# Second MLP of a fused kernel: ScalarE alone empties the product banks, VectorE makes all the splits, and the output weight's sums come one per block product

## The chip, the cores and the metric

The kernel runs on one core of a Trainium2 chip, as one program. The time is the device time of that program in microseconds (us). Before the change it took 1174.68 us, the median of 3 runs (1170.27 to 1175.73). The profiled execution, from which all rows below come, took 1168.19 us; 1166.4 us of it lie between its first and its last instruction (its span).

## The reference, cut to what matters

The program computes three things in a row: attention with RMS norms over 4 batches of 448 tokens, a first MLP without a nonlinearity, and a second MLP. The change touches the second MLP alone. Its reference, for x of 1792 tokens by 768:

```python
h = x @ w_in                      # 768 x 2048
relu6 = np.clip(h + 3.0, 0.0, 6.0)
g = h * relu6 / 6.0
return (g @ w_out).astype(np.float32)   # 2048 x 768
```

## The kernel before, in words

All matmuls run in a reduced-precision type (float32r), so each float32 operand is split in two: a rounded "high" part, made by a ScalarE copy, and the remainder, made by a subtraction of the copy from the original. A product is then three matmuls: high by high, high by low, low by high.

The second MLP works on two pairs of batches (p = 0, then p = 1). Both of its matrix products use Strassen's scheme with seven block products instead of eight. The items of work stand in one list, in the order of `ORDER`. A block, j = 0 to 7 in each pair, has the seven products P1, P2, P6, P5, P7, P3, P4 of x with w_in (nine matmuls of 448 columns each), with the items O2 and O1 of earlier blocks between them (nine matmuls each into six accumulator banks, the tiles `acc`). When all eight blocks of a pair are done, 40 more such `acc` items follow, the rest of the product with w_out. So each pair has 8 x 7 x 9 matmuls into the banks `sA` and `sB`, and 56 x 9 into `acc`.

`sA` and `sB` are used in turn, and a bank's later products are added to what it holds (P6, P7 and P4 add to P1's bank). TensorE may therefore start a product only after the one before it in the same bank has been read out. Some results are read by a ScalarE copy to a tile `u` in SBUF (P1, P6, P5, L1263), some by a VectorE addition straight out of the bank (P2, P7, P3, L1271), and P4 by the two steps of the nonlinearity (`nonlinear`, L1193 on ScalarE and L1194 on VectorE). `gsplit` (L1201) splits what the nonlinearity gives, and `three` and `fourth` (L1225 to L1237) form Strassen's combinations of it on VectorE.

`halves` (L1016) splits the weights (tiles `wt`, 128x384) and the pieces of x (tiles `xo`, 128x448): ScalarE copies, and the subtraction goes to VectorE and GpSimd in turn by the counter `nsplit`, with some weights on VectorE always. `temp` (L1136) forms the sums of w_in (tiles `sx`), and `combos` (L1102) forms the four sums of a w_out block (tiles `G`), all four in one go, and stores them (`sd`) for the 40 later items. `outer` also empties the `acc` banks at the end of a group, partly by VectorE additions out of PSUM.

`prepare` runs six items ahead of the matmuls. The program text is in this order, but a scheduling pass places the instructions on each engine; after that an engine takes its own strictly in order. The loop over the items is the last one below.

```python
    def halves(t, src, alone=False):
        nc.scalar.activation(t[:, 0, :], src, AF.Copy)
        nsplit[0] += 1
        (nc.vector if nsplit[0] % 2 or alone else nc.gpsimd).tensor_sub(t[:, 1, :], src, t[:, 0, :])
```

Of the kernel before, what the change touches and what calls it, by code (L numbers as in the profile page):

```python
# [13 lines left out]
F32 = mybir.dt.float32  # L14
F32R = mybir.dt.float32r
# [3 lines left out]
AF = mybir.ActivationFunctionType  # L19
# [8 lines left out]
P = 128  # L28
# [9 lines left out]
NH = DM // 2  # L38
# [13 lines left out]
def fused_kernel(ctx: ExitStack, tc: tile.TileContext, nat, qT, kT, vin, gq, gk,  # L52
                 w12, w3t, wo, win, wo2, outT):
    nc = tc.nc
# [52 lines left out]
    now = [0]  # L107
# [813 lines left out]
    NWF, NWT, AHEAD2 = 12, 8, 6  # L921
    PAIRS = ((0, 1), (2, 3))
    d1 = ExitStack()
    mp = d1.enter_context(tc.tile_pool(name="m2", bufs=1, side="left", **RW))
    wf, wr, xo = {}, {}, {}
# [81 lines left out]
    def utile():  # L1007
        return mp.tile([P, S], F32, tag="u", bufs=8, name="u")

    def xtile(z, k):  # L1010
        return xo["pool", z in LEFT].tile([P, 2, S], F32R, tag=f"x{z}{k}", name="xo")

    LEFT = ("11", "21", "T2", "T1", "T3")
    nsplit = [0]

    def halves(t, src, alone=False):  # L1016
        nc.scalar.activation(t[:, 0, :], src, AF.Copy)  # L1017
        nsplit[0] += 1
        (nc.vector if nsplit[0] % 2 or alone else nc.gpsimd).tensor_sub(t[:, 1, :], src, t[:, 0, :])
        return t  # L1020

    def xprep(p):
# [59 lines left out]
            items += dn[-2:]  # L1082
        base += 3 * NJ
    wt, sx, once = {}, {}, set()
    wait, puts = [], []

    def drop2(v):
        if v in once:
            drop(v)
        once.add(v)  # L1090

    def combos(j, v1, v2):
        w1, w2 = wf[v1], wf[v2]
        a11, a21 = w1[:, :NH], w1[:, NH:]
        a12, a22 = w2[:, :NH], w2[:, NH:]
        s, t = [], []
        for n, op in enumerate((ALU.add, ALU.subtract, ALU.subtract, ALU.subtract)):
            if n % 2 == 0:
                t.append(xo["pool", False].tile([P, 2, S], F32, tag="G", bufs=M2 // 2, name="G"))
            s.append(t[-1][:, n % 2, :NH])  # L1100
            x, y = ((a21, a22), (s[0], a11), (a11, a21), (a12, s[min(n, 1)]))[n]
            nc.vector.tensor_tensor(out=s[n], in0=x, in1=y, op=op)  # L1102
        drop2(v1)
        drop2(v2)

        def keep():
            for n in range(2):
                dma(sd[j, n], t[n][:, :, :NH])
            made.add(j)

        puts.append((now[0] + 3, keep))

    def prepare(i):
        kind, p, j, v, h = items[i]
        front[0] = v if kind == "O" else v[1]
        if kind == "O":
            upto(v)
            c = slice(NH, 2 * NH) if h in "634" else slice(0, NH)
            wt[i] = halves(mp.tile([P, 2, NH], F32R, tag="wt", bufs=NWT, name="wt"), wf[v][:, c], h not in "12")
            if h in "534":  # L1120
                drop(v)
            elif h in "12" and p == 0:
                drop2(v)
                if h == "1":
                    upto(v + 1)
                    wait.append((now[0], partial(combos, j, v, v + 1)))
            elif h in "12":
                drop(v)
            return
        upto(v[1])  # L1130
        a11, a12 = wf[v[0]][:, :NH], wf[v[0]][:, NH:]
        a21, a22 = wf[v[1]][:, :NH], wf[v[1]][:, NH:]

        def temp(z, x, y, op):
            sx[z] = mp.tile([P, NH], F32, tag="sx", bufs=3, name="sx")
            nc.vector.tensor_tensor(out=sx[z], in0=x, in1=y, op=op)  # L1136
            return sx[z]

        if kind == "P6":
            temp("S1", a21, a22, ALU.add)  # L1140
            temp("S2", sx["S1"], a11, ALU.subtract)
        src = dict(P1=a11, P2=a12, P4=a22).get(kind)
        if src is None:
            if kind == "P7":
                src = temp("S3", a11, a21, ALU.subtract)
            elif kind == "P3":
                src = temp("S4", a12, sx["S2"], ALU.subtract)
            else:
                src = sx["S2" if kind == "P6" else "S1"]
        t = mp.tile([P, 2, NH], F32R, tag="wt", bufs=NWT, name="wt")  # L1150
        wt[i] = halves(t, src)
        if h:
            drop(v[0])
            drop(v[1])
# [33 lines left out]
    xo["pool", False] = rp  # L1188
    rp.tile([P, 2, S], F32, tag="G", bufs=M2 // 2, name="G")

    def nonlinear(src, out):
        u = utile()
        nc.scalar.activation(u, src, AF.Relu, bias=half, scale=1.0 / 6.0)  # L1193
        return nc.vector.scalar_tensor_tensor(out=u if out is None else out, in0=u, scalar=1.0, in1=src,  # L1194
                                              op0=ALU.min, op1=ALU.mult), u

    g, done = {}, []
# [3 lines left out]
        done[:] = [nc.scalar.activation(t[:, 0, :], src, AF.Copy), nc.vector.tensor_sub(t[:, 1, :], src, t[:, 0, :])]  # L1201
        g[p, b, q] = t

    def finish(p, j, z, src):

        b, q = (z % 10 - 1), 2 * j + z // 10 - 1
        if b == 0:
            _, u = nonlinear(src, None)
            gsplit(p, 0, q, u)
            X[z] = u  # L1210
            if z == 21:
                wait.append((now[0] + 2, partial(fourth, j)))
        elif z == 22:
            X["b"] = rp.tile([P, 2, S], F32, tag="G", bufs=M2 // 2, name="G")
            nonlinear(src, X["b"][:, 1])
        else:
            _, X[z] = nonlinear(src, None)
            wait.append((now[0] + 2, partial(three, j)))

    X = {}  # L1220
# [20 lines left out]
    swap = [(sA, sB)]  # L1241
    snap = {}
# [12 lines left out]
    def strassen(i):  # L1255
        kind, p, j, _, _ = items[i]
        a, c = swap[0]
        own = c if kind in ("P2", "P5", "P3") else a
        snap["mm"] = product(kind, i, own, kind in ("P1", "P2", "P5"))
        r = own[:, :S]  # L1260
        if kind in ("P1", "P6", "P5"):
            snap[kind] = utile()
            nc.scalar.activation(snap[kind], r, AF.Copy)  # L1263
            return
        if kind == "P4":
            finish(p, j, 21, r)
            swap[0] = (c, a)
            return
        s, z = {"P2": ("P1", 11), "P7": ("P5", 22), "P3": ("P6", 12)}[kind]
        s = snap.pop(s)  # L1270
        nc.vector.tensor_add(s, r, s)  # L1271
        finish(p, j, z, s)

    acc = {}

# [23 lines left out]
    def outer(i):  # L1299
        _, p, j, _, h = items[i]  # L1300
        if not acc:
            for n in range(KD):
                acc[n] = bank(TAGS[1 + n // 2], "acc")
        low = 3 * (h in "253")
        w = wt.pop(i)
        x = g.pop((p, 0, 2 * j + int(h) - 1) if h in "12" else (p, h, j))
        first, end = j == 0 and h in "1253", j == NJ - 1
        for n in range(3):
            ps, ns = acc[low + n][:, :S], slice(n * P, n * P + P)
            with tc.issue_after(snap["mm"].ins) if i >= turn[p] - 2 else ExitStack():  # L1310
                for a, (y, z) in enumerate(((0, 0), (0, 1), (1, 0))):
                    nc.tensor.matmul(ps, w[:, y, ns], x[:, z, :], start=first and a == 0, stop=end and a == 2,  # L1312
                                     skip_group_check=h in "674")
        if not end:
            return
        b1, b2 = PAIRS[p]

        def put(n, b, t):
            dma(outT[n * P : n * P + P, b * S : b * S + S], t)

        for n in range(3):
            ps = acc[low + n][:, :S]
            if h == "1":
                snap["c", n] = utile()
                nc.scalar.activation(snap["c", n], ps, AF.Copy)
            elif h == "2":
                t = snap["c", n]
                nc.vector.tensor_add(t, ps, t)
                put(n, b1, t)
            elif h == "6":  # L1330
                snap["o", n] = xtile("22", n).bitcast(F32)
                nc.scalar.activation(snap["o", n][:, 1], ps, AF.Copy)
            elif h == "5":
                t = snap["o", n]
                nc.scalar.activation(t[:, 0], ps, AF.Copy)
                nc.vector.tensor_add(t[:, 1], ps, t[:, 1])
            elif h == "4":
                t = utile()
                if n % 2:
                    nc.vector.tensor_copy(t, ps)  # L1340
                else:
                    nc.scalar.activation(t, ps, AF.Copy)
                put(n + 3, b1, t)
            else:
                t = utile()
                nc.vector.tensor_add(t, ps, snap["o", n][:, int(h == "3")])
                put(n + 3 * (h == "7"), b2, t)

    prep_to(AHEAD2)
    xg = xrest(0)  # L1350
    for i, it in enumerate(items):
# [5 lines left out]
        kind, p = it[:2]  # L1357
# [19 lines left out]
        (outer if kind == "O" else strassen)(i)  # L1377
        while puts and puts[0][0] <= i:
            puts.pop(0)[1]()
        while wait and wait[0][0] <= i:  # L1380
            with tc.issue_after(done[1].ins):
                wait.pop(0)[1]()
# [47 lines left out]
```

## Time and profile before

| what | value |
|---|---|
| median of 3 runs | 1174.68 us |
| profiled execution, its time | 1168.19 us |
| its span | 1166.4 us |
| TensorE matmul (PE) busy | 1111.8 us, 95% of the span |
| weight loads (PEld) busy | 943.0 us, 81% |
| VectorE (DVE) busy | 930.2 us, 80% |
| ScalarE (ACT) busy | 778.7 us, 67% |
| GpSimd (POOL) busy | 297.9 us, 26% |
| mean granted TensorE clock | 0.997 of full speed |

The second MLP's matmuls begin at 732.15 us and end near the end of the span, so it takes the last 434 us. A matmul's recorded time (367 ns or so) overlaps the next one's; the pace of a dense stream is read from how far apart the weight loads start, or from a long stretch divided by its matmuls. Each row of waits names the engine and line that waited, and after the arrow the engine and line whose end released it, then the total in us, the number of waits and the longest one. In rows of groups, "x16 | 12.1, 754 | 0.0" means 16 instructions, 12.1 us busy together, 754 ns each on average, and the engine's idle time just before them.

### The profile page before, as it was taken

Reading aid. Unit: us, or ns where it says so; the run is one execution under the profiler, and the core shown is the slowest. Engines: PE = TensorE matmul, PEld = TensorE weight load, DVE = VectorE, ACT = ScalarE, POOL = GpSimd, SP = SyncE. Lnnn points to the kernel's source line nnn. Section 1 sums busy time; section 2 is a strip of 40 time slices with the busy share of each in tenths; the row PEclk is TensorE's granted clock in tenths of the full one; section 3 lists DMA queues with packets and bytes.
Section 4 is the critical chain, followed back from the end, with each engine's and each line's share of the span. In section 5 each row is a group of like instructions: output and inputs, shape, how many; then the busy total and the mean of one; then the engine's idle time right before and its main releaser. Section 6 shows DMA issues by size and latency. Waiting matters only on the chain.

```text
span 1166.4 us, 17544 instructions
## 1 busy us (share of the span) xinstructions
PE 1111.8 (95%) x5483; PEld 943.0 (81%) x5483; DVE 930.2 (80%) x1956; ACT 778.7 (67%) x1645; POOL 297.9 (26%) x249
## 2 busy tenths in 40 slices
PE   5899899899999999999999999899999989999998
PEld 2455576788789888788999899889889879999997
DVE  6869888989788898878874436898989997777764
ACT  6988968898678878777764434545556755555663
POOL 1132322645322213222102004423310253222000
PEclk9999999999999999999999999999999999999999
DMA  8989744789999889898689987654459954434961
GB/s 263 341 273 292 255 142 151 239 285 285 331 309 339 280 295 316 271 314 281 232 295 338 398 315 278 233 194 176 153 205 402 355 174 149 150 129 163 349 230 72
DMA packets 109662, 299.05 MB, mean 256 GB/s; under 512 B 13280, under 2 KB 46048, under 8 KB 109568
## 3 DMA queue, kind: packets, MB, share of 16 engines
q1 hardware_dynamic: 109568, 297.93, 74.4%
q8 instruction: 43, 0.70, 0.3%
q14 instruction: 51, 0.42, 0.1%
HBM read 230.61 MB, written 67.27 MB: 255 GB/s over the span
## 4 chain that ended last, share of the span: by engine, by line
PE 46%; DVE 21%; DMA 16%; ACT 11%; issue 5%; POOL 1%; SPq 0%; ACTq 0%; DVEq 0%; POOLq 0%
PE acc L1312 11%; PE sA L1251 5%; PE sB L1251 5%; PE bank L395 5%; PE bank L256 4%; DMA raw<-in_wo_dram 3%; DMA nat<-in_nat_dram 3%; PE bank L400 2%; DVE PP L638 2%; PE bank L657 2%; ACT PP L650 2%; PE bank L91 2%; PE bank L89 2%; PE bank L90 2%; DVE xl L676 2%
## 5 line engine op out<-in xcount | busy, mean ns | idle before, releaser
L1312 PE MATMUL acc<-g,wt 128*128 128x448 f32 x1008 | 217.0, 368 | 2.5 <-DVE g L1201 2.2
L1312 PEld LDWEIGHTS acc<-g,wt 128*128 128x128 f32 x1008 | 189.1, 188 | 21.8 <-DVE g L1201 3.5
L395 PE MATMUL bank<-xhl,ws 128*128 128x448 f32 x768 | 180.9, 367 | 2.4 <-ACT bs L371 1.2
L395 PEld LDWEIGHTS bank<-xhl,ws 128*128 128x128 f32 x768 | 143.6, 188 | 15.8 <-ACT bs L416 1.6
L650 ACT ACTIVATE PP<-PP,mx 112x448 f32<-112x448 f32 x192 | 127.0, 663 | 36.5 <-DVE mx L645 32.9
L638 DVE CUSTOM_DVE_ANT_0 PP<-bank,rb,rq 112x448 f32<-112x448 f32 x192 | 128.6, 674 | 12.9 <-PE bank L632 10.1
L1251 PE MATMUL sA<-xo,wt 128*128 128x448 f32 x504 | 114.2, 371 | 9.0 <-DVE u L1271 7.8
L256 PE MATMUL bank<-woh,w 128*128 128x384 f32 x256 | 98.6, 509 | 15.3 <-DVE woh L155 12.8
L1251 PE MATMUL sB<-xo,wt 128*128 128x448 f32 x504 | 112.6, 367 | 0.0
L1251 PEld LDWEIGHTS sA<-xo,wt 128*128 128x128 f32 x504 | 94.8, 190 | 20.6 <-DVE u L1271 11.1
L1251 PEld LDWEIGHTS sB<-xo,wt 128*128 128x128 f32 x504 | 93.9, 188 | 10.1 <-DVE u L1271 1.6
L657 PEld LDWEIGHTS bank<-ident,PP 112*128 112x128 f32 x672 | 78.2, 141 | 28.7 <-issue 7.5
L676 DVE TENSOR_TENSOR xl<-bank,xh 128x448 fp32r<-128x448 f32 x142 | 86.9, 615 | 16.5 <-ACT xh L666 15.4
L666 ACT ACTIVATE xh<-bank 128x448 fp32r<-128x448 f32 (+1 forms) x156 | 82.4, 536 | 25.9 <-PE bank L657 23.0
L152 DVE SCALAR_TENSOR_TENSOR raw<-raw 128x384 int32<-128x384 int32 (+1 forms) x112 | 69.4, 620 | 37.4 <-ACT raw L150 33.4
L657 PE MATMUL bank<-ident,PP 112*128 112x112 f32 x672 | 94.4, 262 | 3.4 <-DVE xl L676 2.5
L400 PE MATMUL bank<-xhl,ws 128*128 128x448 f32 x384 | 94.7, 366 | 0.0
L149 ACT ACTIVATE raw<-raw 128x384 f32<-128x384 f32 (+1 forms) x112 | 63.6, 568 | 40.7 <-DMA raw<-in_wo_dram 16.2
L1017 ACT ACTIVATE wt<-wf 128x384 fp32r<-128x384 f32 x160 | 79.2, 514 | 15.1 <-PE sB L1251 6.8
L631 PE MATMUL bank<-K,Q 128*112 128x448 f32 x192 | 79.9, 417 | 5.9 <-DVE mx L638 5.9
L256 PEld LDWEIGHTS bank<-woh,w 128*128 128x128 f32 x256 | 48.8, 196 | 43.8 <-DVE woh L155 16.0
L612 POOL TENSOR_TENSOR K<-kr,K 128x448 fp32r<-128x448 f32 x48 | 59.7, 1264 | 77.5 <-ACT K L610 65.1
(146 smaller groups left out, 2275.7 us busy)
## 6 DMA issues: line engine op xcount, KB each, us to landing
ws<-w12d SPq DMA_DIRECT2D x48, 768.0 KB
ws<-wpd SPq DMA_DIRECT2D x32, 768.0 KB
wf<-wfd SPq DMA_DIRECT2D x56, 384.0 KB
raw<-in_wo_dram SPq DMA_DIRECT2D x44, 384.0 KB
td<-G SPq DMA_DIRECT2D x32, 448.0 KB
G<-td SPq DMA_DIRECT2D x32, 448.0 KB
raw<-in_w_dram SPq DMA_DIRECT2D x32, 384.0 KB
w12d<-ws SPq DMA_DIRECT2D x16, 768.0 KB
```

The costliest lines, as they stand in the source:

```text
L256: nc.tensor.matmul(ps[:, :NH], W["w3"][a, c // 4][:, cs], W["woh"][c, n], start=c == 0, stop=c == M1 - 1)
L395: nc.tensor.matmul(ps[:, :S], w[:, 0, ks], x[:, y, :], start=k == 0 and y == 0, stop=False)
L400: nc.tensor.matmul(ps[:, :S], w[:, 1, ks], L["xhl"][i][:, 0, :], start=False, stop=k == KD - 1)
L631: nc.tensor.matmul(ps[:CP, :S], qs, k1[:, j, :], start=True, stop=False)
L638: anchors[8 * i + s].append(nc.vector.tensor_tensor_reduce(out=T["PP", i][:, c, sl], in0=ps[:CP, :S], in1=T["rb", i][:, sl], op0=ALU.mult, ...
L650: anchors[8 * i + s].append(nc.scalar.activation(v, v, AF.Exp, bias=T["m", i][:, 8 + s : 9 + s], accum_out=T["sum", i][:, s : s + 1]))
L657: nc.tensor.transpose(ps[:, c * CP : c * CP + CP], src[:, c, kb * P : kb * P + P], ident[:CP, :CP])
L666: nc.scalar.activation(hi, ps, AF.Copy)
L676: nc.vector.tensor_sub(lo, ps, hi)
L1017: nc.scalar.activation(t[:, 0, :], src, AF.Copy)
L1251: mm = nc.tensor.matmul(ps[:, :S], w[:, a, ks], x[:, c, :], start=first and k == 0 and n == 0, stop=k == KD // 2 - 1 and n == 2, skip_grou ...
L1312: nc.tensor.matmul(ps, w[:, y, ns], x[:, z, :], start=first and a == 0, stop=end and a == 2, skip_group_check=h in "674")
```

## The change

Five edits, all in the second MLP.

1. `halves` has no counter any more: VectorE makes every remainder, and GpSimd has no work in this part.
2. In `strassen` ScalarE copies each of the seven products out of its bank into a `u` tile. The additions of P2, P7 and P3 and both steps of P4's nonlinearity then read SBUF. `nonlinear` is handed the tile for its intermediate instead of taking one.
3. In `outer` each finished `acc` bank is likewise copied by ScalarE, and VectorE's additions read the copy.
4. `combos` is a generator: its four sums are emitted one after each item of the list, not four at once, each placed behind the latest `gsplit`.
5. The two weight tiles that `combos` reads are given back, and its sums stored, as many items later.

```diff
-    def halves(t, src, alone=False):
+    def halves(t, src):
         nc.scalar.activation(t[:, 0, :], src, AF.Copy)
-        nsplit[0] += 1
-        (nc.vector if nsplit[0] % 2 or alone else nc.gpsimd).tensor_sub(t[:, 1, :], src, t[:, 0, :])
+        nc.vector.tensor_sub(t[:, 1, :], src, t[:, 0, :])
...
-            s.append(t[-1][:, n % 2, :NH])
-            x, y = ((a21, a22), (s[0], a11), (a11, a21), (a12, s[min(n, 1)]))[n]
-            nc.vector.tensor_tensor(out=s[n], in0=x, in1=y, op=op)
+            x, y = ((a21, a22), (t[0][:, 0, :NH], a11), (a11, a21), (a12, t[0][:, 1, :NH]))[n]
+            nc.vector.tensor_tensor(out=t[-1][:, n % 2, :NH], in0=x, in1=y, op=op)
+            yield
...
-                    wait.append((now[0], partial(combos, j, v, v + 1)))
+                    sums.append(combos(j, v, v + 1))
...
         r = own[:, :S]
+        c = utile()
+        nc.scalar.activation(c, r, AF.Copy)
         if kind in ("P1", "P6", "P5"):
-            snap[kind] = utile()
-            nc.scalar.activation(snap[kind], r, AF.Copy)
+            snap[kind] = c
             return
         if kind == "P4":
-            finish(p, j, 21, r)
-            swap[0] = (c, a)
+            finish(p, j, 21, c, utile())
+            swap[0] = swap[0][::-1]
             return
...
-        nc.vector.tensor_add(s, r, s)
-        finish(p, j, z, s)
+        nc.vector.tensor_add(s, c, s)
+        finish(p, j, z, s, c)
...
+            t = utile()
+            nc.scalar.activation(t, ps, AF.Copy)
+            if h == "2":
+                nc.vector.tensor_add(t, t, snap["c", n])
+            elif h in "73":
+                nc.vector.tensor_add(t, t, snap["o", n][:, int(h == "3")])
+            put(n + 3 * (h in "74"), b2 if h in "73" else b1, t)
...
+        with tc.issue_after(done[1].ins) if done else ExitStack():
+            while sums and next(sums[0], 0) == 0:
+                sums.pop(0)
```

The scheduling pass gives a new order on each engine. The first place is VectorE in the middle of pair 0, around the four sums of one block of w_out (`G<-wf` and the like) and the two additions of P7 and P3 behind them (`u<-sA,u` and `u<-sB,u` before, `u<-u` now). Before:

```order
L1201 TENSOR_TENSOR g<-u,g 128x448
L1237 TENSOR_TENSOR u<-u,G 128x448
L1102 TENSOR_TENSOR G<-wf 128x384 x2
L1102 TENSOR_TENSOR G<-G,wf 128x384
L1102 TENSOR_TENSOR G<-wf,G 128x384
L1019 TENSOR_TENSOR wt<-sx,wt 128x384
L1136 TENSOR_TENSOR sx<-wf,sx 128x384
L1136 TENSOR_TENSOR sx<-wf 128x384
L1271 TENSOR_TENSOR u<-sA,u 128x448
L1136 TENSOR_TENSOR sx<-sx,wf 128x384
L1271 TENSOR_TENSOR u<-sB,u 128x448
```

and the same place now:

```order
L1197 TENSOR_TENSOR g<-u,g 128x448
L1233 TENSOR_TENSOR u<-u,G 128x448
L1098 TENSOR_TENSOR G<-wf 128x384 x2
L1016 TENSOR_TENSOR wt<-sx,wt 128x384
L1098 TENSOR_TENSOR G<-G,wf 128x384
L1016 TENSOR_TENSOR wt<-sx,wt 128x384
L1133 TENSOR_TENSOR sx<-wf,sx 128x384
L1098 TENSOR_TENSOR G<-wf,G 128x384
L1133 TENSOR_TENSOR sx<-wf 128x384
L1268 TENSOR_TENSOR u<-u 128x448
L1016 TENSOR_TENSOR wt<-sx,wt 128x384
L1133 TENSOR_TENSOR sx<-sx,wf 128x384
```

The four sums are loosened by weight splits, of which there are more; the addition of P7 still stands behind all four, but it no longer reads a bank.

The second place is ScalarE where the second MLP begins: the first block's copies out of `sA` and `sB`, and the six copies of pieces of x that are split late (`xo<-wr`). Before:

```order
L1263 ACTIVATE u<-sA 128x448
L1017 ACTIVATE wt<-wf 128x384
L1017 ACTIVATE xo<-wr 128x448 x6
L1017 ACTIVATE wt<-sx 128x384
L1193 ACTIVATE u<-u,half 128x448
L1263 ACTIVATE u<-sA 128x448
L1017 ACTIVATE wt<-sx 128x384
L1263 ACTIVATE u<-sB 128x448
```

and now:

```order
L1258 ACTIVATE u<-sA 128x448
L1015 ACTIVATE wt<-wf 128x384
L1015 ACTIVATE xo<-wr 128x448 x6
L1258 ACTIVATE u<-sB 128x448
L1015 ACTIVATE wt<-sx 128x384
L1258 ACTIVATE u<-sA 128x448
L1015 ACTIVATE wt<-sx 128x384
L1189 ACTIVATE u<-u,half 128x448
L1258 ACTIVATE u<-sB 128x448
```

P2's result, which VectorE read out of `sB` before, is now copied by ScalarE behind those six copies.

## Rows read from the trace of the kernel before

**Rows 1.** Busy time by stretch: us, PE, PEld, DVE, ACT, POOL, PEclk, DMA share, GB/s

```profile
732.10:750.00 17.90, 14.60 (x66) 12.89 (x65) 15.42 (x22) 10.91 (x22) 8.81 (x7) 0.90 0.79 293
750.00:866.00 116.00, 111.41 (x539) 99.77 (x538) 101.77 (x162) 59.30 (x118) 33.70 (x29) 1.00 0.48 171
866.00:958.50 92.50, 88.92 (x428) 79.59 (x426) 87.05 (x144) 60.42 (x128) 23.30 (x16) 1.00 0.85 313
958.50:1082.70 124.20, 124.15 (x604) 113.08 (x605) 96.91 (x159) 69.57 (x136) 34.09 (x31) 1.00 0.45 155
1082.70:1166.40 83.70, 79.99 (x388) 72.42 (x386) 52.22 (x97) 43.80 (x89) 0.00 (x0) 1.00 0.58 213
```

**Rows 2.** Chain that ended last: start us, us, what; its last piece on TensorE

```profile
1082.71 79.99 PE acc L1312 x387
```

**Rows 3.** Waits of the weight loads, 732.1 to 1166.4 us

```profile
PEld sA L1251 <- DVE u L1271: 11.1, 9, 3.7
PEld acc L1312 <- DVE g L1201: 3.5, 3, 2.2
PEld sB L1251 <- DVE u L1271: 1.6, 6, 0.3
PEld sA L1251 <- ACT u L1263: 1.5, 1, 1.5
PEld acc L1312 <- ACT g L1201: 0.6, 1, 0.6
PEld sB L1251 <- ACT u L1263: 0.4, 1, 0.4
```

**Rows 4.** Waits of the weight loads, 750 to 866 us

```profile
PEld sA L1251 <- DVE u L1271: 6.6, 6, 2.0
```

**Rows 5.** Timeline, 722 to 752 us: start, us, engine, line, [idle before <- releaser]

```profile
735.26 2.91 ACT L1017 ACTIVATE xo<-wr 128x448 fp32r<-128x448 f32 x6
...
735.91 7.74 POOL L1019 TENSOR_TENSOR xo<-wr,xo 128x448 fp32r<-128x448 f32 x6 [4.82 <-ACT xo L1017]
...
746.92 3.01 PEld L1251 LDWEIGHTS sA<-xo,wt 128*128 128x128 f32 x9 [3.68 <-DVE u L1271]
```

**Rows 6.** Timeline, 779.5 to 784.5 us

```profile
778.84 1.38 DVE L1102 TENSOR_TENSOR G<-wf 128x384 f32<-128x384 f32 x1
...
782.72 0.62 DVE L1271 TENSOR_TENSOR u<-sA,u 128x448 f32<-128x448 f32 x1
...
783.39 1.12 PEld L1251 LDWEIGHTS sA<-xo,wt 128*128 128x128 f32 x6 [2.03 <-DVE u L1271]
```

**Rows 7.** Groups of VectorE by form, 750 to 866 us

```profile
L1019 DVE TENSOR_TENSOR wt<-wf,wt 128x384 fp32r<-128x384 f32 x16 | 12.1, 754 | 0.0
...
L1227 DVE TENSOR_TENSOR G<-G,u 128x448 f32<-128x448 f32 x7 | 6.8, 968 | 0.0
...
L1271 DVE TENSOR_TENSOR u<-sB,u 128x448 f32<-128x448 f32 x9 | 5.5, 611 | 0.0
```

**Rows 8.** Groups of VectorE by form, 1100 to 1166.4 us, without GpSimd

```profile
L1019 DVE TENSOR_TENSOR wt<-wf,wt 128x384 fp32r<-128x384 f32 x27 | 14.9, 552 | 0.0
```

**Rows 9.** Timeline of VectorE, 1090 to 1096 us, without GpSimd

```profile
1093.01 0.56 DVE L1019 TENSOR_TENSOR wt<-wf,wt 128x384 fp32r<-128x384 f32 x1
1093.48 0.62 DVE L1201 TENSOR_TENSOR g<-G,g 128x448 fp32r<-128x448 f32 x1
1094.02 0.56 DVE L1019 TENSOR_TENSOR wt<-wf,wt 128x384 fp32r<-128x384 f32 x1
```

**Rows 10.** Groups of GpSimd, 700 to 1166.4 us, first and last of four

```profile
L1019 POOL TENSOR_TENSOR wt<-wf,wt 128x384 fp32r<-128x384 f32 x37 | 43.2, 1169 | 94.3 <-ACT wt L1017 91.4 <-DVE wt L1019 1.5 <-DVE G L1227 1.4
...
L1019 POOL TENSOR_TENSOR xo<-wr,xo 128x448 fp32r<-128x448 f32 x12 | 16.0, 1357 | 10.1 <-ACT xo L1017 9.0 <-DMA out_dram<-u 1.1
```

**Rows 11.** Groups of ScalarE by form, 750 to 866 us

```profile
L1193 ACT ACTIVATE u<-u,half 128x448 f32<-128x448 f32 x19 | 12.7, 671 | 20.8 <-DVE u L1271 20.6
...
L1263 ACT ACTIVATE u<-sB 128x448 f32<-128x448 f32 x11 | 5.8, 532 | 1.6 <-PE sB L1251 1.6
```

More of the change, by code (lines that the diff above doesn't have):

```diff
@@ L1013, in fused_kernel @@
     LEFT = ("11", "21", "T2", "T1", "T3")
-    nsplit = [0]
-    def halves(t, src, alone=False):
+    def halves(t, src):
         nc.scalar.activation(t[:, 0, :], src, AF.Copy)
-        nsplit[0] += 1
-        (nc.vector if nsplit[0] % 2 or alone else nc.gpsimd).tensor_sub(t[:, 1, :], src, t[:, 0, :])
+        nc.vector.tensor_sub(t[:, 1, :], src, t[:, 0, :])
         return t
@@ L1084, in fused_kernel @@
     wt, sx, once = {}, {}, set()
-    wait, puts = [], []
+    wait, puts, sums = [], [], []
     def drop2(v):
@@ L1095, in combos @@
         a12, a22 = w2[:, :NH], w2[:, NH:]
-        s, t = [], []
+        t = []
         for n, op in enumerate((ALU.add, ALU.subtract, ALU.subtract, ALU.subtract)):
@@ L1118, in prepare @@
             c = slice(NH, 2 * NH) if h in "634" else slice(0, NH)
-            wt[i] = halves(mp.tile([P, 2, NH], F32R, tag="wt", bufs=NWT, name="wt"), wf[v][:, c], h not in "12")
+            wt[i] = halves(mp.tile([P, 2, NH], F32R, tag="wt", bufs=NWT, name="wt"), wf[v][:, c])
             if h in "534":
@@ L1189, in fused_kernel, with nonlinear @@
     rp.tile([P, 2, S], F32, tag="G", bufs=M2 // 2, name="G")
-    def nonlinear(src, out):
-        u = utile()
+    def nonlinear(src, out, u):
         nc.scalar.activation(u, src, AF.Relu, bias=half, scale=1.0 / 6.0)
@@ L1202, in gsplit, with finish @@
         g[p, b, q] = t
-    def finish(p, j, z, src):
+    def finish(p, j, z, src, u):
         b, q = (z % 10 - 1), 2 * j + z // 10 - 1
         if b == 0:
-            _, u = nonlinear(src, None)
+            nonlinear(src, None, u)
             gsplit(p, 0, q, u)
@@ L1214, in finish @@
             X["b"] = rp.tile([P, 2, S], F32, tag="G", bufs=M2 // 2, name="G")
-            nonlinear(src, X["b"][:, 1])
+            nonlinear(src, X["b"][:, 1], u)
         else:
-            _, X[z] = nonlinear(src, None)
+            _, X[z] = nonlinear(src, None, u)
             wait.append((now[0] + 2, partial(three, j)))
@@ L1325, in outer @@
                 nc.scalar.activation(snap["c", n], ps, AF.Copy)
[L1326 to L1333, printed above, removed]
-                t = snap["o", n]
[L1335 to L1347, printed above, removed]
+                continue
+            if h in "65":
+                if h == "6":
+                    snap["o", n] = xtile("22", n).bitcast(F32)
+                t = snap["o", n]
+                nc.scalar.activation(t[:, int(h == "6")], ps, AF.Copy)
+                if h == "5":
+                    nc.vector.tensor_add(t[:, 1], t[:, 0], t[:, 1])
+                continue
+            t = utile()
[5 more added lines that the diff above has]
+            put(n + 3 * (h in "74"), b2 if h in "73" else b1, t)
     prep_to(AHEAD2)
```

## The prediction

> **What bounds the kernel now.** I read the busy time by stretch first. The second MLP runs from 732 us to the end in five stretches: its first block, the rest of pair 0's blocks, pair 0's 40 later items with the preparation of pair 1, pair 1's blocks, and its 40 later items [rows 1]. The reader is to see that PE is busy nearly all the time in all of them, that DVE stands at 86 to 94% up to 958 us, ACT at 51 to 65%, and that POOL works in four of the five.
>
> Next comes TensorE's own pace. The last stretch has no waits to speak of: 387 matmuls in 79.99 us, 0.2067 us each [rows 2]. The second MLP has 2016 matmuls, so 416.7 us is what they cost without a wait. None is added or removed, and that floor stays.
>
> So only the waits can be won, and the third view prices them: the weight loads of the second MLP waited 11.1 + 3.5 + 1.6 + 1.5 + 0.6 + 0.4 = 18.7 us [rows 3]. Of that, 12.7 us are waits for a VectorE addition that reads a bank (L1271), 3.5 us for VectorE's half of a g split. By place: 3.7 us in one wait in the first block [rows 5], 6.6 us in six waits in the rest of pair 0 [rows 4], 4.1 us before `acc` matmuls (3.5 + 0.6), and the other 4.3 us in small ones. After the wait of 3.7 us nine weight loads took 3.01 us where nine at pace take 9 x 0.2067 = 1.86, so it cost 1.2 us more [rows 5]; the granted clock of that stretch is 0.90, against 1.00 in the others [rows 1], so part of it ran at the lower level of 1.2 GHz after an idle TensorE. All that can be won is therefore 18.7 + 1.2 = 19.9 us.
>
> **Why VectorE is late.** In the last stretch, where POOL does nothing, a weight split takes 552 ns [rows 8] and dense instructions start 0.47 us (128x384) and 0.54 us (128x448) apart [rows 9]. In pair 0's blocks the same split takes 754 ns and the subtraction L1227 takes 968 ns, while the addition out of `sB` takes 611 ns [rows 7]. What is stretched has two SBUF inputs; what reads a bank is not. Over all forms, DVE took 101.77/162 = 0.628 us an instruction there and 52.22/97 = 0.538 us without POOL [rows 1]: 0.09 x 162 = 14.6 us of VectorE's time in 116 us go into being held up, with 29 POOL splits in that stretch, or 0.5 us for each.
>
> The Trainium skill, "SBUF — State Buffer", section "SBUF: two separate sides", says that GpSimd and VectorE share a pair of ports as an exclusive lock, which binds a VectorE operation with two SBUF inputs against a GpSimd one that reads SBUF. The trace agrees: 754 against 552 ns for the one kind, 611 for the other.
>
> **The change part by part.**
>
> *Splits from GpSimd to VectorE.* 93 subtractions go over (four groups, 37 in the first, 12 in the last) [rows 10]. In pair 0's blocks it is 29; at 0.47 us apart VectorE gets 13.6 us more, at their full 552 ns 16.0 us, and it loses the 14.6 us of being held up. So its load there stays where it is, 101 to 103 us of 116. I take zero for the load. What does change is the kind of delay: no instruction is stretched to 1.4 us any more, and a split that took GpSimd 1169 ns is done in 552.
>
> *Copies out of the banks.* Four more per block, so 64, and 20 more at the ends of the `acc` groups: 84 x 0.532 us = 44.7 us [rows 11] on ScalarE. In pair 0's rest that is about 7 blocks x 4 x 0.532 = 14.9 us on top of 59.3 us in 116 us, or 64%; the engine has the room. VectorE saves nothing by it: an addition out of a bank takes 611 ns and one from two SBUF tiles is about as long as the g split's 0.62 [rows 7, 9]. The gain is in when the bank is free: after a copy that waits for the product alone, and no longer after an addition behind VectorE's queue.
>
> The rule that speaks against this is in the Trainium skill, "VectorE: DVE Perf Modes", section "Rules for kernel authors": work on a matmul's output from PSUM at the slow rate, and copy it to SBUF first only if many operations follow. Here one follows (two for P4). By that rule 44.7 us of ScalarE are spent for no VectorE time, and the trace agrees that no VectorE time is saved; if ScalarE had no idle time to hide them the sum would turn to the slower side, but it has over 40 us idle in that stretch alone.
>
> What is queued behind a waiting copy on ScalarE is everything else it does for TensorE: the high halves of the weights and of g. ScalarE already stands idle 20.6 us in pair 0's blocks in front of the nonlinearity's first step, for a VectorE addition [rows 11], and a copy behind that step in the queue inherits its wait. The trace has no row for this as it will be. Its nearest rows are the waits of TensorE for ScalarE's copies, 0.4 us at one place and 1.5 us at another out of 48 copies [rows 3]; for each of 16 blocks I bound it by 0 and 0.4 us, so 0 to 6.4 us in all, and take 0.15 us a block, near the mean of those rows: 2.4 us lost.
>
> *The four sums of w_out.* Before, they stood in a row on VectorE. At 778.84 the first took 1.38 us, held up by GpSimd, and the addition that frees `sA` started at 782.72; the weight load waited 2.03 us for it [rows 6]. Now splits stand between the sums, P7's addition stands behind all four still, but the bank it used to free is free by then. The weights' tiles are given back four items later; nothing waits for these tiles in rows 3 or 4, so I cost that at nothing.
>
> *First block.* At 735.91 GpSimd works on six pieces of x for 7.74 us, VectorE falls behind, and the addition for P7 comes so late that P4 waits 3.68 us [rows 5]. VectorE takes those six now at 0.54 us, 3.2 us. New there: P2's copy stands behind six ScalarE copies that end at 735.26 + 2.91 = 738.2, so it ends at 738.7. P5, which wants that bank, would start at 732.15 + 3 x 1.86 = 737.7. I leave 1.1 us of wait: won 3.7 + 1.2 - 1.1 = 3.8 us.
>
> *The sum.* First block 3.8. Rest of pair 0: 6.6 us go, and I leave 2.0 for weights that come late from a VectorE that is still 88% loaded: 4.6. Waits before `acc`: VectorE is at 87.05/92.5 = 94% there and stays so, POOL's 16 splits being turned over like for like; I leave half: 2.1. The small waits: I leave 2.6 of 4.3: 1.7. Together 12.2, less 2.4 for ScalarE: 9.8, say 10 us. At the very end one of three copies moves from VectorE to ScalarE; they come a third of an accumulator group apart, so nothing is added. The profiled execution took 1168.2 us, which would become 1158; the median shown is 1174.7, 6.5 above it, and by that measure the forecast is **1164.7 us**.
>
> **The rivals.**
>
> *The wait moves to ScalarE's queue.* VectorE's additions stay as late as before, since its load is unchanged. The steps that wait for them stand in ScalarE's queue ahead of bank copies, and TensorE waits for ScalarE instead. For it: the 20.6 us of idle time [rows 11], and DVE at 88 to 94%. Against it: an addition may now be late by the length of two products before it stops TensorE. Then only the first block's 3.8 us and little else are won, less 2.4: about 2 us, 1172.7 us.
>
> *VectorE overflows; slower.* If its instructions keep their mean of 0.628 us with GpSimd gone, the hold-up being of another cause, pair 0's rest needs (162 + 29) x 0.628 = 120 us, and with half of its present idle 14.2 us 127: 11 us more than now. The next stretch needs (144 + 16) x 87.05/144 = 96.7 us against 92.5, so 4 more. Less the first block and the small waits (3.8 + 1.7) and with ScalarE's 2.4 that is 12 us lost, some 1186 us. It decides from a mean of 116/191 = 0.607 us up. Against it stand the 552 ns without POOL [rows 8]; for it, that such a dense stretch without POOL isn't in the trace.
>
> *All waits leave.* By the lock's rule taken to its end, without a stretched instruction VectorE keeps ahead of TensorE everywhere: 19.9 us won, 1154.8 us. Against it: 88% load leaves little to catch up with.
>
> **How the numbers follow.** Forecast (6 to 15 us won) 0.52; wait moved to ScalarE (0 to 6 us won) 0.26; VectorE overflows 0.12; all waits leave 0.10. A measurement of this kernel can tell 0.5% from no change, 5.9 us here. Faster by more is the first and the last case: 0.62; within it 0.26; slower by more 0.12. The range goes from all waits gone, 1155, to slightly above no change, 1177, which takes in ScalarE's upper bound of 6.4 us with the first block alone won; what lies outside is most of the slower case and a little at the low end.
>
> **What would show it.** Right: the weight loads' waits for a bank are for ScalarE's copies and sum to under 5 us in pair 0; weight splits on VectorE fall to about 0.55 us in every stretch; VectorE's busy time in the whole second MLP stays within 10 us of before; the 3.7 us wait and the lowered clock behind it are gone. Wrong: weight-load waits above 15 us in all, whoever they are for; splits still at 0.65 us or more; or VectorE busy without a break in pair 0 with TensorE waiting for `wt` or `g`.

## The result and the profile after

| | before | after |
|---|---|---|
| median, 4 runs each | 1174.53 us (1170.27 to 1175.73) | 1156.27 us (1154.74 to 1162.08) |
| profiled execution | 1168.19 us | 1154.90 us |
| second MLP, first to last weight load | 430.0 us | 418.0 us |

The ratio is 0.986, with a 95% interval of 0.9817 to 0.9903. A second timing of the same kernel, six runs, gave 1155.35 us and 0.9856 (0.9826 to 0.9886). The forecast was 1164.7, in a range of 1155 to 1177. By the medians 15 to 18 us are gone where 10 were forecast.

Of the 13.3 us between the two profiled executions, 12.0 lie in the second MLP. The stretches of [rows 1], in the kernel after (us, then busy time of PE, PEld, DVE, ACT, POOL, the granted clock, DMA share, GB/s):

```profile
730.90:748.70 17.80, 17.16 (x84) 15.51 (x84) 15.08 (x30) 13.84 (x29) 0.00 (x0) 1.00 0.83 302
748.70:860.00 111.30, 111.25 (x545) 102.08 (x545) 100.93 (x197) 71.70 (x145) 0.00 (x0) 1.00 0.55 191
860.00:947.00 87.00, 84.84 (x409) 76.21 (x408) 78.77 (x153) 63.82 (x137) 0.00 (x0) 1.00 0.89 322
947.00:1070.00 123.00, 122.93 (x602) 112.78 (x602) 101.66 (x189) 82.92 (x167) 0.00 (x0) 1.00 0.46 154
1070.00:1153.10 83.10, 79.39 (x384) 71.59 (x382) 50.81 (x95) 47.79 (x99) 0.00 (x0) 1.00 0.58 213
```

GpSimd has no work left there. VectorE does 35 instructions more in the second stretch and is busy no longer: 100.93/197 = 0.512 us each, against 0.628 [rows 1]. ScalarE carries 280.1 us over the five stretches, 36 more than before. The granted clock of the first stretch is 1.00, and was 0.90.

The waits of the weight loads in the kernel after, all of the second MLP (total, number, longest; before, 18.7 us in [rows 3]):

```profile
PEld acc L1309 <- ACT g L1197: 1.9, 2, 1.4
PEld sB L1247 <- ACT u L1258: 1.9, 3, 1.0
PEld sA L1247 <- ACT u L1258: 1.5, 1, 1.5
PEld acc L1309 <- DVE g L1197: 0.6, 2, 0.4
```

They sum to 5.9 us. No bank is waited for on VectorE's account any more; all four waits of the banks are for ScalarE's copies (L1258). In the second stretch the six waits with 6.6 us [rows 4] are gone; the one left there, 0.4 us at its end for a copy out of `sB`, was there before too [rows 3].

Groups of VectorE in that stretch, kernel after (those of [rows 7], now at other lines):

```profile
L1016 DVE TENSOR_TENSOR wt<-wf,wt 128x384 fp32r<-128x384 f32 x33 | 17.9, 553 | 1.7 <-ACT wt L1015 1.5
L1268 DVE TENSOR_TENSOR u<-u 128x448 f32<-128x448 f32 x21 | 13.1, 623 | 2.9 <-ACT u L1258 2.6
L1223 DVE TENSOR_TENSOR G<-G,u 128x448 f32<-128x448 f32 x7 | 4.3, 618 | 0.0
```

The split fell from 754 to 553 ns, the subtraction of `three` from 968 to 618, and the addition, now of two SBUF tiles, went from 611 to 623.

Waits of ScalarE in the same stretch, kernel after:

```profile
ACT u L1258 <- PE sB L1247: 13.5, 15, 1.6
ACT u L1258 <- PE sA L1247: 12.6, 12, 1.5
...
ACT u L1189 <- DVE u L1268: 1.7, 3, 0.7
```

Before, ScalarE stood idle 20.6 us for VectorE's additions [rows 11]; now 1.7. It waits for TensorE's products instead, which is waiting ahead of time.

The first block in the kernel after, timeline (start, us, what, idle before), for [rows 5]:

```profile
734.01 2.91 ACT L1015 ACTIVATE xo<-wr 128x448 fp32r<-128x448 f32 x6
...
734.62 3.30 DVE L1016 TENSOR_TENSOR xo<-wr,xo 128x448 fp32r<-128x448 f32 x6
...
736.82 0.53 ACT L1258 ACTIVATE u<-sB 128x448 f32<-128x448 f32 x1
...
737.41 1.71 PEld L1247 LDWEIGHTS sB<-xo,wt 128*128 128x128 f32 x9 [1.01 <-ACT u L1258]
```

P2's copy stands behind six copies of x on ScalarE, so P5 waits 1.01 us; VectorE does the six splits in 3.30 us, where GpSimd took 7.74. Nine loads then take 1.71 us, so no low clock follows. The longest wait left is where pair 1 begins, and has the same shape, three `acc` copies ahead of a bank's. It is as long as before (1.5 us [rows 3]):

```profile
943.61 1.42 ACT L1333 ACTIVATE u<-acc 128x448 f32<-128x448 f32 x3 [0.21 <-PE acc L1309]
...
944.90 0.56 ACT L1258 ACTIVATE u<-sA 128x448 f32<-128x448 f32 x1
...
945.51 1.71 PEld L1247 LDWEIGHTS sA<-xo,wt 128*128 128x128 f32 x9 [1.50 <-ACT u L1258]
```

### The profile page after: what moved, and what is told of

Read it like the earlier page. It is cut to its first block, busy times and chain, and to the rows that moved or that the text cites. A ratio compares the mean times of both kernels' runs of the same rounds, so it can differ in the third digit from the quotient of the medians.

```text
span 1153.1 us, 17490 instructions
## 1 busy us (share of the span) xinstructions
PE 1109.7 (96%) x5483; PEld 944.3 (82%) x5483; DVE 924.0 (80%) x2047; ACT 815.5 (71%) x1729; POOL 185.9 (16%) x156
## 4 chain that ended last, share of the span: by engine, by line
PE 59%; DVE 14%; DMA 12%; ACT 9%; issue 3%; SPq 1%; POOL 1%; ACTq 0%; POOLq 0%; DVEq 0%
PE acc L1309 17%; PE sB L1247 8%; PE sA L1247 8%; PE bank L395 6%; PE bank L256 4%; PE bank L400 3%; DVE PP L638 3%; PE bank L657 2%; DMA raw<-in_wo_dram 2%; DMA rsd<-rss 2%; DVE xl L676 2%; DMA rsb<-rsd 2%; DMA raw<-in_w_dram 2%; DVE raw L152 2%; DVE Q L604 2%
## 5 line engine op out<-in xcount | busy, mean ns | idle before, releaser
L1309 PEld LDWEIGHTS acc<-g,wt 128*128 128x128 f32 x1008 | 189.1, 188 | 20.6 <-ACT g L1197 1.9
L1016 DVE TENSOR_TENSOR wt<-wf,wt 128x384 fp32r<-128x384 f32 x160 | 86.8, 552 | 14.0 <-ACT wt L1015 13.8
```

## The experiments

Two theories stood against each other. A: GpSimd's splits stretch VectorE's instructions, and removing them is what pays. B: what pays is that a bank comes free after a ScalarE copy and no longer after an addition in VectorE's queue. All ratios are to the kernel before on the same chip, with the 95% interval.

**Edit 1 alone** (`splits_only`). The additions still read the banks.

```diff
-        (nc.vector if nsplit[0] % 2 or alone else nc.gpsimd).tensor_sub(t[:, 1, :], src, t[:, 0, :])
+        nc.vector.tensor_sub(t[:, 1, :], src, t[:, 0, :])
```

> The kernel before with the first edit alone: VectorE makes all splits, GpSimd none; banks are still emptied as before. Theory A (GpSimd holds VectorE up, and that is what made bank reads late): most of the gain comes, 10 us or more off, weight splits on VectorE at 0.55 us, weight-load waits of the second MLP from 18.7 to 6 us or less. Theory B (what counts is that a bank is freed without passing VectorE's queue): VectorE has 93 more instructions in the same queue, so only the first block's wait shrinks, 2 to 5 us off, and at least 10 us of waits for bank-reading additions remain.

Measured: 1156.18 us against 1171.88, ratio 0.988 (0.9852 to 0.9908). Its weight loads' waits, and VectorE's group of splits in pair 0:

```profile
PEld sA L1248 <- ACT u L1260: 3.6, 5, 1.4
PEld sB L1248 <- ACT u L1260: 1.6, 2, 0.8
PEld acc L1309 <- ACT wt L1015: 0.4, 1, 0.4
```

```profile
L1016 DVE TENSOR_TENSOR wt<-wf,wt 128x384 fp32r<-128x384 f32 x32 | 17.6, 551 | 6.2 <-ACT wt L1015 6.2
```

Edit 1 alone brings the waits to 5.6 us. VectorE's additions still free banks, and no load waits for one. The edit does two things at once, though: the splits that VectorE now makes also stand between the four sums, and an addition overtakes the last of them (timeline of VectorE, behind two sums at 794.35 us and one at 795.75):

```profile
797.16 0.62 DVE L1268 TENSOR_TENSOR u<-sB,u 128x448 f32<-128x448 f32 x1
797.69 0.55 DVE L1099 TENSOR_TENSOR G<-wf,G 128x384 f32<-128x384 f32 x1
```

How much of the gain is the hold-up and how much the loosened row, this run does not tell; `gpsimd_beside`, below, takes the hold-up by itself. A repeat (`splits_only_again`) gave 0.9878 (0.9852 to 0.9904) and 5.6 us again.

> The first edit alone once more, beside the last one. If the copies add something of their own to the splits, it is 2 to 5 us slower than splits and copies were (0.9844 and 0.9849 of before); if not, its ratio is below 0.987. Its waits are again for ScalarE's copies, 5 to 6 us in sum.

**Edits 2 and 3 alone** (`copies_only`): GpSimd keeps its splits, the four sums stay in one go.

```diff
+        c = utile()
+        nc.scalar.activation(c, r, AF.Copy)
         if kind in ("P1", "P6", "P5"):
-            snap[kind] = utile()
-            nc.scalar.activation(snap[kind], r, AF.Copy)
+            snap[kind] = c
...
-        nc.vector.tensor_add(s, r, s)
+        nc.vector.tensor_add(s, c, s)
```

> The kernel before with the copies alone: ScalarE empties every bank, GpSimd keeps its 93 splits, the four sums stand in a row. Theory A: little, 0 to 4 us off; splits stay at 0.65 to 0.75 us and the waits move to ScalarE's copies, or to weights, 10 us or more in sum. Theory B: 8 us or more off, waits at 8 us or less although VectorE's instructions stay stretched.

Measured: 1166.69 us, 0.9967 (0.9947 to 0.9987); waits 16.1 us:

```profile
PEld sA L1250 <- ACT u L1261: 7.0, 3, 5.1
PEld sB L1250 <- ACT u L1261: 5.8, 6, 1.3
PEld acc L1312 <- ACT g L1200: 1.8, 2, 1.3
PEld acc L1312 <- DVE g L1200: 1.5, 3, 0.9
```

This is the prediction's first rival: the wait moves to ScalarE's queue. Its longest one in the timeline of this kernel:

```profile
939.39 11.30 POOL L1019 TENSOR_TENSOR xo<-wr,xo 128x448 fp32r<-128x448 f32 x1 [3.46 <-ACT xo L1017]
...
949.13 0.54 DVE L1019 TENSOR_TENSOR wt<-sx,wt 128x384 fp32r<-128x384 f32 x1
...
950.65 4.48 POOL L1019 TENSOR_TENSOR xo<-wr,xo 128x448 fp32r<-128x448 f32 x4
...
955.09 1.01 POOL L1019 TENSOR_TENSOR wt<-sx,wt 128x384 fp32r<-128x384 f32 x1
...
956.13 1.47 DVE L1136 TENSOR_TENSOR sx<-wf,sx 128x384 f32<-128x384 f32 x1 [6.46 <-POOL wt L1019]
...
957.72 0.53 ACT L1017 ACTIVATE wt<-sx 128x384 fp32r<-128x384 f32 x1 [9.41 <-DVE sx L1136]
...
960.24 0.55 ACT L1261 ACTIVATE u<-sA 128x448 f32<-128x448 f32 x1
...
960.85 1.25 PEld L1250 LDWEIGHTS sA<-xo,wt 128*128 128x128 f32 x4 [5.07 <-ACT u L1261]
```

One split of x holds GpSimd for 11.30 us; the four behind it take 4.48 us together. During that one VectorE runs 20 instructions back to back, none longer than 0.61 us, and GpSimd gets done 1.0 us after VectorE has run out of them. Here it is GpSimd that is held up. The split of a weight sum comes late behind these; VectorE waits 6.46 us for that one, ScalarE's copy of the next weight sum waits 9.41 us for VectorE, and the bank's copy stands behind it. A product that ended long ago is not read out because of a queue three engines long.

**The whole change without edit 1** (`copies_sums`).

```diff
-        nc.vector.tensor_sub(t[:, 1, :], src, t[:, 0, :])
+        (nc.vector if nsplit[0] % 2 or alone else nc.gpsimd).tensor_sub(t[:, 1, :], src, t[:, 0, :])
```

> The changed kernel with the first edit undone: GpSimd makes its 93 splits again, copies and spread sums stay. Theory A: 8 us or more slower than the whole change, that is 4 to 10 us better than before. Theory B: within 4 us of the whole change.

Measured: 1166.54 us, 0.9949 (0.9927 to 0.9971), waits 16.1 us. Undoing edit 1 gives back 0.9949 - 0.986 of 1172 us, some 10 us. The trace's waits are those of the copies alone. That says little of the sums: on VectorE they stand as in `copies_only` in six of their eight groups, since the scheduling pass decides the order.

**The whole change with the four sums in one go** (`splits_copies`), and its repeat.

```diff
-                    sums.append(combos(j, v, v + 1))
+                    wait.append((now[0], partial(combos, j, v, v + 1)))
```

> The changed kernel with the sums of the output weight in one go again. TensorE's order is the same as in the whole change. If a bank no longer waits for a VectorE addition, four sums in a row (2.2 us) delay nobody: within 2 us of the whole change, 16 to 18 us off. If they still do, one wait of 1 to 2 us in some of pair 0's blocks comes back, 4 us or more slower than the whole change.

> Splits and copies with the sums in one go, once more, beside the whole change. If spreading the sums is worth nothing, the two are within 2 us of each other; the pace of the last 387 matmuls is 200.0 ns again if it belongs to the program.

Measured: 1153.24 us, 0.9849 (0.9824 to 0.9874), waits 5.0 us; again 1151.98 us, 0.9844 (0.9816 to 0.9872), waits 4.2 us. Leaving out edits 4 and 5 costs nothing. Here too VectorE's order around the sums differs from the whole change's at the first and the last group alone.

**Edits 4 and 5 alone** (`sums_only`): the four sums one per item, everything else as before. (The tiles go back behind the last sum, so edit 5 comes with edit 4.)

```diff
+            yield
...
+        with tc.issue_after(done[1].ins) if done else ExitStack():
+            while sums and next(sums[0], 0) == 0:
+                sums.pop(0)
```

> The kernel before with the four sums of the output weight spread over four items, GpSimd's splits and bank-reading additions as before. If the burst of sums is what made the 2 us waits before a bank of pair 0, these go: 4 to 6 us off, waits from 18.7 to about 13 us. If the burst only showed a VectorE that was late anyway, within 2 us of before and waits of 17 us or more.

Measured: 1167.52 us, 0.997 (0.9949 to 0.9991); waits 17.2 us, led by these two; and, in the second fence, the timeline of this kernel at the wait that I had put down to the four sums (783.39 us before, [rows 6]), with VectorE's sums ahead of it:

```profile
PEld sA L1251 <- DVE u L1271: 11.4, 10, 3.7
PEld acc L1312 <- DVE g L1201: 3.2, 3, 1.5
```

```profile
779.32 1.84 DVE L1101 TENSOR_TENSOR G<-wf 128x384 f32<-128x384 f32 x2
...
781.08 0.55 DVE L1101 TENSOR_TENSOR G<-G,wf 128x384 f32<-128x384 f32 x1
...
781.66 0.56 DVE L1101 TENSOR_TENSOR G<-wf,G 128x384 f32<-128x384 f32 x1
...
784.34 1.71 PEld L1251 LDWEIGHTS sA<-xo,wt 128*128 128x128 f32 x9 [2.07 <-DVE u L1271]
```

The wait stays, at 2.07 us, but the run does not test what it was made for. The program text spreads the sums; on VectorE they still stand in a row here, in the order of before, and only the first and the last of the eight groups come out otherwise. What a row of four sums costs by itself is not shown by any run.

**GpSimd kept busy beside the whole change** (`gpsimd_beside`): 93 subtractions of a tile from itself on GpSimd, where the 93 splits were, into a tile that nothing reads. TensorE, VectorE and ScalarE do the same in the same order as in the whole change, instruction for instruction in the two traces, the loosened sums included; and in the list of its waits no engine waits for GpSimd.

```diff
+        if not (nsplit[0] % 2 or alone):
+            n = t.shape[2]
+            j = mp.tile([P, S], mybir.dt.bfloat16, tag="idle", bufs=1, name="idle")
+            nc.gpsimd.tensor_sub(j[:, :n], t[:, 0, :], t[:, 0, :])
```

> The whole change, and beside it GpSimd makes 93 subtractions that nobody reads, as many as it made before, each of the high half of a split from itself into a small scratch tile. The order on PE, VectorE and ScalarE is that of the whole change, instruction for instruction. If the hold-up of VectorE by GpSimd is the cause, VectorE's two-SBUF-input instructions stretch again (mean in pair 0's blocks from 0.55 and 0.62 us to 0.63 us or more over all), VectorE now has the splits and the hold-ups, and the time goes up by 10 us or more, to no better than before or even slower. If the hold-up is no cause and only the place of the splits mattered, the time stays within 3 us of the whole change.

The whole change, timed beside it on the same chip:

> The whole change once more, for a comparison in the same call. 14 to 18 us off. If the pace of the dense stream of 387 matmuls at the end (206.7 ns a matmul in its first profile, 200.0 in that of the kernel with splits and copies) belongs to the program, it is 206.7 again; if it belongs to the execution, it may be either.

Measured: 1178.54 us against 1155.35 for the whole change, so 23 us for work that nobody waits for; to the kernel before the ratio is 1.0062 (1.0037 to 1.0087). Waits 29.3 us. Three views of this kernel: the largest waits of the weight loads; pair 0's blocks by engine; and VectorE's groups over the whole second MLP.

```profile
PEld sB L1254 <- ACT u L1265: 12.5, 10, 2.1
PEld sA L1254 <- ACT u L1265: 10.5, 10, 2.6
```

```profile
755.00:870.00 115.00, 107.25 (x508) 95.75 (x507) 111.65 (x190) 67.34 (x137) 45.11 (x28) 0.99 0.49 170
```

```profile
L1018 DVE TENSOR_TENSOR wt<-wf,wt 128x384 fp32r<-128x384 f32 x158 | 97.9, 631 | 2.5 <-ACT wt L1017 2.5
...
L1275 DVE TENSOR_TENSOR u<-u 128x448 f32<-128x448 f32 x48 | 34.1, 710 | 0.9 <-ACT u L1265 0.9
...
L1230 DVE TENSOR_TENSOR G<-G,u 128x448 f32<-128x448 f32 x16 | 14.9, 930 | 0.0
```

VectorE is busy 97% of pair 0's blocks, 0.588 us an instruction. Over the 0.512 of the whole change that is 0.076 x 190 = 14.4 us for 28 GpSimd instructions, 0.5 us for each. The addition L1275 settles what is stretched: with a bank as one input it took 611 ns beside GpSimd's work [rows 7], and with two SBUF inputs it takes 710 ns here, and 623 where GpSimd is idle. That is the Trainium skill's rule in "SBUF — State Buffer", section "SBUF: two separate sides", that GpSimd and VectorE lock each other out of a shared pair of ports when a VectorE operation has two SBUF inputs; the runs agree with it. Only GpSimd's work is new in this kernel, so beside a VectorE that makes all the splits this work alone is enough to make the waits. Theory A accounts for the greater part of the gain; what B's copies add is in the next section.

**Four of the six late pieces of x behind P2's copy** (`late_x`, on `splits_copies`), against the 1.0 us left in the first block.

```diff
+            if i == 2:
+                snap["late"] = snap["out"]
+            if 2 <= i < 7:
+                es.enter_context(tc.issue_after(snap["late"].ins))
```

> Splits and copies, sums in one go, and four of the six late pieces of x split only after P2's bank copy, so that ScalarE reaches that copy about 2 us earlier. If the wait of 1.0 us in the first block is due to the six copies ahead of P2's, it goes, and the waits of the second MLP fall from 4.3 to 5.0 us to 3 to 4 us; the time is within 2 us of splits and copies, too little to be told apart by time.

Measured: 1154.12 us, 0.9834 (0.981 to 0.9857), waits 4.3 us. P5 no longer waits, and the product behind it does (timeline of this kernel):

```profile
743.19 1.72 PEld L1247 LDWEIGHTS sA<-xo,wt 128*128 128x128 f32 x9 [0.57 <-ACT u L1258]
```

Half of it comes back, which the time cannot tell from `splits_copies`. The best ratios are these two, 0.9834 to 0.9849; their intervals overlap that of the whole change.

## Why the prediction was right, and where its sizes were off

**VectorE's load.** Right. 93 splits came to it (some of them ahead of the second MLP's first matmul), and its busy time went from 353.4 to 347.3 us in the five stretches and from 930.2 to 924.0 us in all: what the splits add, the end of the hold-up gives back. The 0.5 us that the prediction put on each GpSimd split is what `gpsimd_beside` measures. What I missed is what that buys: a VectorE with an equal busy share and no stretched instruction is on time. The prediction kept half of the `acc` waits on the ground of a load of 94%, and 2.0 us in pair 0's rest on that of 88%; the loads are 91% in both stretches now, and TensorE waits for VectorE 0.6 us in the whole second MLP.

**The sum by its terms**, in the profiled executions:

| term | forecast won | measured won |
|---|---|---|
| first block | 3.8 | 3.7 + 1.2 - 1.0 = 3.9 |
| rest of pair 0 | 4.6 | 6.6 |
| before `acc` | 2.1 | 4.1 - 2.5 = 1.6 |
| small waits | 1.7 | 4.3 - 2.4 = 1.9 |
| new waits for ScalarE | -2.4 | in the rows above |

The mechanism held; one size did not. What was too high is what VectorE would still be late by: in the rest of pair 0 I left 2.0 us for it and half of the `acc` waits besides, and 0.6 us came in all. The waits for VectorE fell from 16.2 to 0.6 us. Those for ScalarE rose from 2.5 to 5.3 us, so it costs 2.8 us, where the forecast had 3.5 (2.4, and the 1.1 left in the first block, which came out at 1.0): that size was about right. By place, as in the table, these waits stand in the other rows, 1.0 us in the first block, 1.3 before `acc` and 0.5 among the small ones.

The measured terms give 14.0 us; the second MLP got 12.0 shorter. The 2 us between are in no wait: in the second profile of the same program, with the same 5.9 us of waits, the second MLP took 415.6 us, 14.4 less than before. The floor of 416.7 us that the prediction put under the waits was too high, since before took 430.0 - 19.9 = 410.1 us without them; the last stretch's pace is not that of the whole. The sum does not use it.

**The median.** In the profiled executions 12.0 us of the possible 19.9 in the second MLP went, near the forecast's 10. The medians make it look like the rival in which all waits leave (1154.8 against 1156.27), but 5.9 us of waits are still there. The 15 to 18 us by the medians are at or above the upper end of the 6 to 15 that the prediction gave its own case, and that the median came out inside the range, 1.3 us from its end, owes something to luck. The difference is in how each profiled execution stands to its own median: before 6.3 us under it, after 1.4. Part of that may be the clock: 51 runs of before have a mean granted clock of 0.9941, the 10 of the whole change 0.9961, and 0.2% of 1160 us is 2.3 us. Part may be the program ahead of the second MLP, which no edit is about and whose end varies by 9 us from profile to profile (last section). No profile of a slower execution of before was taken, so neither is shown.

**The four sums.** Open. The prediction read two things from one row, four sums on end and one of them held up by GpSimd (the one of 1.38 us is the second of the four, not the first). `sums_only` leaves both as they were at that place, and edit 1 removes both, so the share of each in the 6.6 us is not known; that the hold-up is enough is shown by `gpsimd_beside`, where the sums stand loosened. What loosens them is edit 1, as `splits_only` shows; edits 4 and 5 bring some 3 us alone (1 to 6 by the interval), without a known cause, and nothing on top of the others.

**Copies out of the banks.** Right that they save no VectorE time (611 to 623 ns an addition) and that ScalarE has the room: 84 instructions more cost it 36 us of busy time, under the 44.7 forecast. Their gain, the bank free earlier, is small: some 4 us alone (2 to 6 by the interval). On top of edit 1 they take the waits from 5.6 to 5.0 or 4.2 us and the ratio from 0.988 to 0.9849 or 0.9844; side by side on one chip the means of six runs are 1157.3 us for edit 1 and 1153.7 with the copies. So some 3 to 4 us are likely, of which the waits hold 1.4 us at most; the rest is in no wait, and its cause is open. Pair 0's rest gains by them (3.6 of `splits_only`'s 5.6 us lie there), the first block loses (0.2 us of wait there in `splits_only`, 1.0 with the copies).

**The rivals.** That the wait moves to ScalarE's queue is what happens if GpSimd keeps its splits (`copies_only`): 16.1 of 18.7 us of waits stay, 12.8 of them for bank copies. I had made VectorE's load the condition; it is GpSimd's work, and the longest of these waits begins with a GpSimd instruction that VectorE held up. That VectorE overflows needs the extra splits and the hold-up together, as `gpsimd_beside` has them: 0.588 us an instruction, a little under the 0.607 from which I let it begin, and 1178.5 us where I had 1186.

## What to carry to other kernels

An instruction given to a helper engine costs more than its own time: price it by what it does to the engine that shares its memory. Here each split on GpSimd took VectorE 0.5 us, and VectorE does the whole split in 0.55, so the helper took next to nothing off. The price can fall on the helper too: beside a VectorE that never paused, one of its splits took 11.3 us instead of 1.1. When an engine is late, compare the mean time of one instruction where its neighbour is idle and where it works, before looking for a burst to spread. When an experiment moves instructions in the program text, look at their order on the engine before reading its time: here a scheduling pass had put most of them back. A wait left over after a mend belongs to one term of the sum: name whose it is before adding a term for the new owner.

## What the runs showed that was not expected

The same matmuls at the same granted clock do not always run at one pace. First the profile of the whole change, then the second profile of the same program; each with the last run of `acc` matmuls in TensorE's timeline and a stretch of 40 us out of it:

```profile
1069.05 80.47 PE L1309 MATMUL acc<-g,wt 128*128 128x448 f32 x387
```

```profile
1090.00:1130.00 40.00, 40.00 (x195) 36.38 (x195) 25.27 (x48) 24.35 (x51) 0.00 (x0) 1.00 0.61 224
```

```profile
1074.83 78.03 PE L1309 MATMUL acc<-g,wt 128*128 128x448 f32 x387
```

```profile
1090.00:1130.00 40.00, 40.00 (x202) 37.54 (x201) 25.73 (x48) 24.82 (x52) 0.00 (x0) 1.00 0.77 283
```

The 387 matmuls took 80.47 us in one and 78.03 in the other, each with one wait of some 0.5 us, at a granted clock of 1.00. What differs is not in the program, and its cause is open. The part ahead of the second MLP, whose matmuls are the same in all kernels, ended between 728 and 738 us in the profiles. So the second MLP's own length, first to last weight load, tells the kernels apart better than the whole time does. Two profiles of one program agree in it to 3 us or better; waits came out at 5.9 us both times.

| kernel | second MLP, us |
|---|---|
| before | 430.0 |
| `sums_only` | 427.8 |
| `copies_sums` | 427.1 |
| `copies_only` | 426.8 |
| `splits_only` and its repeat | 417.8, 417.8 |
| the whole change, twice | 418.0, 415.6 |
| `splits_copies` and its repeat | 412.8, 415.8 |
| `late_x` | 413.9 |
| `gpsimd_beside` | 437.0 |

After an idle TensorE the clock is lower. After the wait of 5.07 us in `copies_only`, by stretch:

```profile
955.18:960.85 5.67, 0.97 (x6) 0.56 (x4) 4.66 (x5) 3.13 (x8) 4.47 (x4) 0.85 0.22 71
960.85:963.96 3.11, 3.11 (x8) 2.81 (x9) 2.07 (x4) 1.87 (x4) 1.07 (x1) 0.50 0.94 269
```

The granted clock is 0.50, that is 1.2 GHz, and nine loads take 3.11 us where nine at 1.00 take 1.84 a few microseconds later. After waits of 1.0 and 1.5 us in the kernel after, nine took 1.71. In these traces, then, one long wait cost more than several short ones of the same sum.
